# Attention with a window and sinks, then a gated MLP, on one core: another order of TensorE's groups, another load order, and other constants in the planner

## The chip, the core and the metric

The kernel runs on one core of one Trainium2 chip. The metric is the device time of one execution in microseconds, as the median over several runs. The profile is of one further execution; its span runs from the first to the last instruction of the program that the profiler recorded.

## What is computed

Four batches of eight heads, 768 tokens each, 64 channels per head. A token attends to the first four tokens (the sinks) and to the 128 tokens up to itself. The result, 3072 tokens of 512 channels, goes through an MLP with 2048 hidden channels whose gate is h * sigmoid(beta * h).

```python
scores = scale * np.matmul(q, k.transpose(0, 1, 3, 2))
is_sink = pos[None, :] < int(n_sink)
rel = pos[:, None] - pos[None, :]
keep = is_sink | ((rel >= 0) & (rel < int(window)))
scores = np.where(keep, scores, -1000000000.0)
a = np.exp(scores - np.max(scores, axis=-1, keepdims=True))
a = a / (np.sum(a, axis=-1, keepdims=True) + 1e-09)
x = np.matmul(a, v)            # then heads side by side: (3072, 512)
h = x @ w_in                   # (3072, 2048)
g = h * (1.0 / (1.0 + np.exp(-beta * h)))
out = g @ w_out                # (3072, 512)
```

Inputs and output are float32; the kernel multiplies in bfloat16.

## The kernel before

The tokens are cut into eight half-batches of 384. A half-batch has four units, one for each pair of heads. For the first two half-batches (`XB` is 2) TensorE transposes q and k, by identity products (function `T`, L697), and also transposes the attention output (`OT`, L880). For the other six a transposing DMA on SyncE does both (`XT` L734, `XO` L891).

One unit goes through these steps. Loads of q, k and v land in float32 staging tiles, of which each name has two (L635). Casts make bfloat16 of them, on VectorE, ScalarE or GpSimd (L558, L560, L563). Score products use 64 rows of the array, so those of the two heads run side by side (`SC`, L783). ScalarE takes the exponential (L792); masks are multiplied on VectorE (L803, L809) or selected on GpSimd (L798). The sinks' scores for later tokens have a product and an exponential of their own (`SS`, L819, L823), whose keys GpSimd gathers (L725). The attention-value products (`AV`, L851, L861) carry a column of ones, so that the row sums come with them; VectorE takes the reciprocal (L866) and normalises (L868).

The MLP has two products. The first (`HQ`, L910) makes 128 hidden channels of 384 tokens in four matmuls of 384 columns; ScalarE takes a tanh (L915) and VectorE forms the gate product (L917). The second (`OQ`, L931) accumulates 128 tokens of output over 16 matmuls of 512 columns in four groups. A copy with a factor of one half brings the result to SBUF, on ScalarE (L558) or VectorE (L564), and SyncE stores it (L940). The weights arrive in sixteen pieces of 512 KB (`load_w`, L647) and are cast, too.

Nothing is issued in the order in which this code stands. Each operation is recorded in a graph with its engine or choice of engines, an assumed duration, and what it reads and writes. TensorE's work is recorded in groups, each with a letter: T transposes, C and D the two halves of a unit's scores, S sinks, A attention-value, X output transposes, h and g the two halves of four first-product matmuls in the first two half-batches, H the same in the others, O a quarter of an output tile, b the transpose of beta. The string `ORDER` says in which order the groups come. The list `PAR['l0']` permutes the eleven loads of the first half-batch; the string `PAR['mix']` says how the loads of the next two half-batches (a) and the weight pieces (w) alternate. Loads are chained in that order on SyncE's queue.

`schedule` then walks in an assumed time. The next TensorE group, in the given order, and the next operation of every other engine compete by the earliest assumed start. Where several are ready on an engine, the one with the longest tail goes first. Where an operation can run on several engines, the one that would end first takes it, with a handicap for ScalarE (`BIAS` until `EARLY`). `place` gives each operation its assumed end, and each DMA an issue, a place in the stream and a landing. Where TensorE would idle before the assumed time 48 us (`FILL_TO`), `fillers` puts in products of ones (L1027), whose length is the assumed gap; up to 4.9 us they are assumed to run at half speed. What comes out of the walk is fixed: each engine's list, its engine choices, the PSUM banks and the fillers. On the chip each engine runs its list in order and waits on semaphores only.

Of the kernel before, what the change touches and what calls it, by code (L numbers as in the profile page):

```python
# [22 lines left out]
PAR = {'MD': 1, 'XB': 2, 'l0': [0, 2, 6, 1, 3, 4, 9, 5, 7, 10, 8], 'mix': 'aawwaawawawwawwaaaawwawwawwwawaa'}  # L23
ORDER = ('TCDTSTTDCSDSCASCTADACbXXAhhhXXThghDghgDhggThgggChhgghgShDSghSghghTghgCASCAXADOXOAhhhhXOXOgOOggOOhghg'
         'hhgOOOghgghghhhghgOgOSDgSChCOghSgADODCCOODOOSAAOAOSSOCCSOSODCHHHHHHHHOHDDOHAHDCHHAHHHAAOODDOOOODCDOH'
         'SCCHHOOASSHHOHOHHHHHSHHHAACSHSOHDCCOAODDOOCCDOAOOHHSHSAOHHOHAAHHHHHHHSHOHOHOSSOCDOHDCCOHHAOOHHHHHSHH'
         'HOSOCCDOHHOHODDAHOAHAOODCCASOOOCDDHHHHHHOAOHOOSHHOOSAHHAOHHHHHOOOHHHHOOHHHHHHOOHHHHOHOOOOOHOOOOOOOOO'
# [10 lines left out]
class Op:  # L38
    __slots__ = ("eng", "fn", "deps", "signal", "count", "waits", "sem", "vc", "dma", "seq", "end", "ns", "alts",
                 "group", "tail", "preds", "left", "succ", "at", "queue", "ring", "lag", "x", "tag", "chain")  # L40
# [6 lines left out]
class Graph:  # L47
# [4 lines left out]
    LEAD, PAD, LATE = 1500, 2000, 90000  # L52
    BIAS, EARLY = 300, 100000
    FILL_TO = 48000
    RING, FETCH, SWITCH = 165, 900, 85
    DEPTH = 9

    def __init__(self):
        self.ops = []
        self.groups = []  # L60
        self.writers = {}
        self.readers = {}
        self.last_load = None
        self.filler = None
# [7 lines left out]
    def add(self, eng, fn, ns=0, r=(), w=(), x=(), dma=None, alts=None, queue=470, ring=64, lag=0, after=(), tag=None):  # L72
# [4 lines left out]
        o.queue, o.ring, o.lag, o.x, o.tag, o.chain = queue, ring, lag, list(x), tag, None  # L77
# [28 lines left out]
    def place(self, o, at):  # L106
        o.at = at
        if o.dma:
            self.pending = [x for x in self.pending if x[0] > at]
            issued, need = at + o.queue + 40, min(o.ring, self.RING)  # L110
            total = sum(n for _, n in self.pending)
            for f, n in self.pending:
                if total + need <= self.RING:
                    break
                issued, total = max(issued, f), total - n
            begin = issued + o.lag if o.lag else at + 1150 + o.ns
            self.dma_free = max(self.dma_free + o.ns, begin)
            self.pending.append((self.dma_free, o.ring))
            self.free[o.eng] = issued
            o.end = self.dma_free + 950 + (self.PAD if at > self.LATE else 0)  # L120
        else:
            if o.eng == "pe":
                self.n_pe += 2
                if self.n_pe >= self.fetched + 256:
                    self.fetched += 256
                    self.dma_free = max(self.dma_free, at) + self.FETCH
                rows = o.group is not None and o.group.tag in "CD"
                if rows != self.rows:
                    at = o.at = at + self.SWITCH
                    self.rows = rows  # L130
            self.free[o.eng] = at + o.ns
            o.end = at + o.ns + self.LAT[o.eng]
# [15 lines left out]
    def schedule(self, order):  # L148
# [47 lines left out]
        self.dma_free, self.pending, self.n_pe, self.rows, self.fetched = 0.0, [], 0, False, 0  # L196
# [40 lines left out]
        while at_pe < len(todo) or pool:  # L237
# [20 lines left out]
            for o in pool:  # L258
                opts = []
                for e, (fn, ns) in o.alts.items():  # L260
# [5 lines left out]
                    if o.dma:  # L266
# [188 lines left out]
def _program(nc, G, sb, ps, q, k, v, w_in, w_out, beta, out):  # L455
# [274 lines left out]
    def XT(hb, i):  # L730
# [5 lines left out]
            x16[n][hb % NX][:, cs[0]:cs[0] + len(cs), :, :].rearrange("p c h d -> p (c h d)")), 1500,  # L736
            r=[(n + "16", hb % NX, j, c_) for j in range(4) for c_ in cs],
            w=[("qkT", hb % (NT // 4), j, i, c_) for j in range(4) for c_ in cs], dma=f"dx{n}{hb % 2}", queue=1540, ring=999, lag=1350)
# [25 lines left out]
    def SC(u):  # L764
# [23 lines left out]
        for j, grp in enumerate(gs):  # L788
# [5 lines left out]
            for kind_, sg in (("d", 1), ("p", -1)):  # L794
                at_ = [i for i, blk in enumerate(grp) if blk[0] == kind_]
                if at_:
# [5 lines left out]
                    if UNITS[u][0] < PAR.get('MD', 2):  # L802
                        alts["dve"] = (lambda e, d=d, mk=mk: e.tensor_tensor(d, d, mk, ALU.mult),  # L803
                                       70 + 256 * len(at_) / 1.9)
                    any_of(alts, r=[("E", z, j), ("maskT", int(kind_ == "p"))], w=[(kind_, z, j)])
            if grp[0][0] == "s":
# [3 lines left out]
                any_of({"gp": (fn, 1150), "dve": (fn, 335)}, r=[("E", z, j), "maskS"], w=[("s", z, j)])  # L810
# [252 lines left out]
```

The softmax here doesn't subtract the row's maximum and nothing guards it: scores larger than these inputs give would overflow.

## Time and profile before

| | |
|---|---|
| median of 5 runs | 226.73 us (226.5 to 227.06) |
| profiled execution, its own time | 227.1 us |
| its span | 225.4 us |
| TensorE busy | 217.8 us |
| VectorE busy | 142.2 us |
| ScalarE busy | 141.9 us |
| GpSimd busy | 67.0 us |
| first product of the MLP, 512 matmuls (L910) | 92.8 us busy, 326 ns mean |
| second product, 400 matmuls (L931) | 93.1 us busy, 371 ns mean |
| fillers, 31 matmuls (L1027) | 10.6 us busy |
| DMA | 40.95 MB, 182 GB/s on average |

Busy time is the union of the intervals in which instructions of a group were in flight. Consecutive matmuls overlap in flight, so a group's mean is longer than the spacing at which its matmuls are issued; the spacing is read from the starts in the timeline. "Idle before" is the engine's idle time just ahead of an instruction, followed by what released it.

### The profile page before, as it was taken

To read this page: it belongs to the slowest core of one execution; us is meant where nothing else is said; L and a number is where in the kernel's file an instruction comes from. 1 tells how busy PE (TensorE), PEld (TensorE's weight loads), DVE (VectorE), ACT (ScalarE), POOL (GpSimd) and SP (SyncE) were. 2 spreads that over 40 slices of the span, in tenths; PEclk is the share of its full clock that TensorE was granted. 3 is DMA by queue.
4 is the path that set the end of the run, shared out by engine and by line. 5 is a ranking of instruction groups with operands and counts; after the bars stand their busy time and mean duration, and the time that the engine had idled before them with its cause. 6 is when DMAs were issued, how large, how long until landed. Compare 5 with 4: busy or idle time off the path is not lost.

```text
span 225.4 us, 4484 instructions
## 1 busy us (share of the span) xinstructions
PE 217.8 (97%) x1720; PEld 119.5 (53%) x1720; DVE 142.2 (63%) x313; ACT 141.9 (63%) x257; POOL 67.0 (30%) x157
## 2 busy tenths in 40 slices
PE   8987999999999999999999999999999999999994
PEld 2544555555455445645564665455455556555443
DVE  2898899878758279839775478757362626455100
ACT  2595998145782767547788847778756756566221
POOL 7274344100363526352108510141435400000000
PEclk9999999999999999999999999999999999999999
DMA  7999979996999999899999999994133032101112
GB/s 161 266 345 373 351 188 348 344 248 126 216 204 213 226 203 235 192 251 223 202 237 203 201 224 220 247 242 118 47 84 81 0 84 81 49 4 47 47 47 93
DMA packets 104741, 40.95 MB, mean 182 GB/s; under 512 B 93312, under 2 KB 97680, under 8 KB 104720
## 3 DMA queue, kind: packets, MB, share of 16 engines
q1 hardware_dynamic: 103152, 40.65, 78.1%
q8 instruction: 13, 0.21, 0.4%
q10 hardware_dynamic: 1568, 0.02, 0.4%
q14 instruction: 8, 0.07, 0.1%
HBM read 27.30 MB, written 6.29 MB: 149 GB/s over the span
## 4 chain that ended last, share of the span: by engine, by line
PE 70%; DVE 10%; SPq 9%; DMA 9%; ACT 1%; issue 1%
PE P L931 32%; PE P L910 28%; SPq L635 6%; DVE g L917 4%; DMA wst<-in_moe_w_in_dram 4%; PE P L861 4%; PE P L783 3%; DMA k_stage<-in_k_dram 3%; DMA v_stage<-in_v_dram 2%; PE P L851 1%; DVE k L563 1%; DVE w_in L563 1%; SPq L891 1%; PE P L819 1%; DVE qkT L563 1%
## 5 line engine op out<-in xcount | busy, mean ns | idle before, releaser
L931 PE MATMUL P<-w_out,g 128*128 128x512 bf16 (+2 forms) x400 | 93.1, 371 | 0.1
L910 PE MATMUL P<-xT,w_in 128*128 128x384 bf16 x512 | 92.8, 326 | 0.3 <-DVE xT L563 0.3
L915 ACT ACTIVATE t<-P,hbeta 128x384 f32<-128x384 f32 x128 | 71.8, 587 | 31.7 <-PE P L910 24.5
L917 DVE SCALAR_TENSOR_TENSOR g<-t,P 128x384 bf16<-128x384 f32 x128 | 68.1, 550 | 35.2 <-ACT t L915 32.3
L798 POOL TENSOR_SCALAR_AFFINE_SELECT E<-E 128x256 bf16<-128x256 bf16 (+1 forms) x109 | 52.8, 516 | 57.6 <-ACT E L792 57.4
L910 PEld LDWEIGHTS P<-xT,w_in 128*128 128x128 bf16 x512 | 48.3, 98 | 35.2 <-issue 0.8
L931 PEld LDWEIGHTS P<-w_out,g 128*128 128x128 bf16 x400 | 36.6, 98 | 37.1 <-issue 1.1
L792 ACT ACTIVATE E<-P 128x768 bf16<-128x768 f32 (+1 forms) x64 | 45.6, 761 | 14.1 <-PE P L783 13.8
L861 PE MATMUL P<-vaug,E 128*128 128x65 bf16 x352 | 18.6, 193 | 0.7 <-DVE E L803 0.4
L558 ACT ACTIVATE osb<-P 128x512 f32<-128x512 f32 (+2 forms) x16 | 9.1, 571 | 15.3 <-PE P L931 15.1
L861 PEld LDWEIGHTS P<-vaug,E 128*128 128x128 bf16 x352 | 16.5, 97 | 3.9 <-ACT E L792 0.7
L868 DVE TENSOR_TENSOR onorm<-P,rden 128x384 bf16<-128x384 f32 x32 | 17.5, 553 | 0.5
L783 PE MATMUL P<-qkT 64*128 64x128 bf16 (+1 forms) x256 | 16.5, 239 | 1.1 <-ACT E L792 0.4
L823 ACT ACTIVATE ES<-P 128x128 bf16<-128x128 f32 (+1 forms) x32 | 12.1, 392 | 7.0 <-PE P L819 7.0
L563 DVE CAST k<-k_stage 128x512 bf16<-128x512 f32 (+1 forms) x24 | 11.8, 494 | 5.3 <-DMA k_stage<-in_k_dram 5.2
L783 PEld LDWEIGHTS P<-qkT 64*128 64x128 bf16 x256 | 8.2, 94 | 12.4 <-issue 4.4
L563 DVE CAST q<-q_stage 128x512 bf16<-128x512 f32 (+1 forms) x19 | 9.6, 504 | 6.5 <-DMA q_stage<-in_q_dram 6.5
L851 PE MATMUL P<-vS,ES 128*128 128x130 bf16 x64 | 12.7, 221 | 0.7 <-DVE vS L686 0.4
L563 DVE CAST vaug<-v_stage 128x512 bf16<-128x512 f32 x18 | 8.0, 442 | 8.0 <-DMA v_stage<-in_v_dram 7.9
L725 POOL TENSOR_TENSOR kS<-qkT,headm 128x8 bf16<-128x8 bf16 x16 | 3.0, 209 | 32.1 <-DMA qkT<-k 28.5
L1027 PE MATMUL P<-ones 128*128 128x512 bf16 (+2 forms) x31 | 10.6, 474 | 1.2 <-POOL ones L569 1.1
L564 DVE TENSOR_SCALAR osb<-P 128x512 f32<-128x512 f32 x9 | 6.2, 690 | 6.3 <-PE P L910 2.6
(48 smaller groups left out, 91.0 us busy)
## 6 DMA issues: line engine op xcount, KB each, us to landing
v_stage<-in_v_dram SPq DMA_DIRECT2D x24, 256.0 KB, 4.8
out_dram<-osb SPq DMA_DIRECT2D x23, 256.0 KB, 2.5
q_stage<-in_q_dram SPq DMA_DIRECT2D x18, 256.0 KB, 4.8
k_stage<-in_k_dram SPq DMA_DIRECT2D x18, 256.0 KB, 5.6
wst<-in_moe_w_in_dram SPq DMA_DIRECT2D x5, 512.0 KB, 8.5
wst<-in_moe_w_out_dram SPq DMA_DIRECT2D x4, 512.0 KB, 7.9
g<-in_moe_w_out_dram SPq DMA_DIRECT2D x4, 512.0 KB, 7.1
q_stage<-in_q_dram SPq DMA_DIRECT2D x8, 192.0 KB, 4.6
```

The lines of the kernel that those rows point to most:

```text
L563: return lambda e: e.tensor_copy(dst, at())
L635: o = add("sp", lambda e: e.dma_start(dst, src), ns, w=[("stg", n, z, j) for j in keys], dma=f"d{n}{z}{'' if i is None else i}", ring={610 ...
L783: add("pe", lambda e, dst=dst, own=own, kc=kc, rows=rows, q0=q0, nq=nq: e.matmul(dst(), tokens(own, hp, 1, rows, kc, 1)[:, 0, :], tokens(h ...
L792: add("act", lambda e, src=src, dst_=dst_: e.activation(dst_, src(), AF.Exp, bias=0.0, scale=SCALE), act_ns(256 * n), w=[(k_, z, j) for k_ ...
L798: alts = {"gp": (lambda e, d=d, sg=sg, at_=at_: e.affine_select(d, d, [[0, 2 * len(at_)], [sg, 128]], ALU.is_ge, 0.0, base=min(sg, 0), cha ...
L851: add("pe", lambda e, m=m, o0=o0: e.matmul(A()[:, o0:o0 + 2 * (D + 1)], ES[z][:, (c0 + m) * 128:(c0 + m + 1) * 128], vS[b % 2][:, 2 * hp:2 ...
L861: e.matmul(A()[:, o0:o0 + D + 1], E[z][:, i, hh, :], vaug[vz][:, kb % NK, 2 * hp + hh, :], start=a, stop=o, skip_group_check=True), 39,
L868: add("dve", lambda e: e.tensor_tensor(onorm[:, on, 2 * c0:2 * c1, :], av()[:, :, 0:D], rden[on][:, 0:2 * nb].unsqueeze(2).to_broadcast([1 ...
L910: first = add("pe", lambda e, c=c: e.matmul(hp(), w_in16[:, c, m * 128:(m + 1) * 128], xT[:, hb, c, 128 * c0:128 * c1], start=(c == 0), st ...
L915: add("act", lambda e: e.activation(tt[ti][:, 0:n], hp(), AF.Tanh, bias=0.0, scale=hbeta[:, m:m + 1]), act_ns(n) + 93, r=["hbeta"], w=[("t ...
L917: add("dve", lambda e: e.scalar_tensor_tensor(gt[hb % NG][:, m, 128 * c0:128 * c1], tt[ti][:, 0:n], 1.0, hp(), ALU.add, ALU.mult), dve_ns( ...
L931: add("pe", lambda e, m=m: e.matmul(P[:, bk[0], a:b], gt[hb % NG][:, m, t * 128:(t + 1) * 128], w_out16[:, m, a:b], start=(m == 0), stop=( ...
```

## The change

The order string, the load order and the alternation of loads are replaced. The planner's assumptions are replaced with them: a DMA's issue time now depends on the kind of the one before it (`DMA`, `CLASS`, `last_dma`), each kind has a service time, a queue room and a lag, fetches of instructions stall the assumed DMA stream at listed counts on all engines (`FETCHES`, `SMALL`, `stall`), some assumed durations of masks, attention-value products and transposing loads are altered, and `DEPTH`, `LEAD`, `BIAS` and `EARLY` have other values. A choice of the engine that issues the stores is added (`OUT`), which nothing sets.

The operations on the data are the same in number and size. The built lists differ on all engines: 45 fillers instead of 31; 34 runs of consecutive score groups (C or D) instead of 37; full-size output copies on VectorE 2 instead of 9 and on ScalarE 21 instead of 14; some casts of q, k, v and of weights on other engines; and the order everywhere. The order begins with `TTSCD` instead of `TCDTS`, and the first eleven loads are k1 q3 q1 k0 q0 v0 v1 k3 q2 k2 v2 instead of q0 q1 q3 k0 k1 q2 v1 k2 k3 v2 v0, where the number is a pair of heads for q and k and a block of 128 tokens for v. In TensorE's list the first transpose stands behind 20 fillers of 512 columns and one of 256; before it was behind 12 and one of 384.

```diff
-PAR = {'MD': 1, 'XB': 2, 'l0': [0, 2, 6, 1, 3, 4, 9, 5, 7, 10, 8], 'mix': 'aawwaawawawwawwaaaawwawwawwwawaa'}
-ORDER = ('TCDTSTTDCSDSCASCTADACbXXAhhhXXThghDghgDhggThgggChhgghgShDSghSghghTghgCASCAXADOXOAhhhhXOXOgOOggOOhghg'
-         'hhgOOOghgghghhhghgOgOSDgSChCOghSgADODCCOODOOSAAOAOSSOCCSOSODCHHHHHHHHOHDDOHAHDCHHAHHHAAOODDOOOODCDOH'
-         'SCCHHOOASSHHOHOHHHHHSHHHAACSHSOHDCCOAODDOOCCDOAOOHHSHSAOHHOHAAHHHHHHHSHOHOHOSSOCDOHDCCOHHAOOHHHHHSHH'
-         'HOSOCCDOHHOHODDAHOAHAOODCCASOOOCDDHHHHHHOAOHOOSHHOOSAHHAOHHHHHOOOHHHHOOHHHHHHOOHHHHOHOOOOOHOOOOOOOOO'
+PAR = {'MD': 1, 'XB': 2, 'l0': [3, 6, 2, 1, 0, 8, 9, 7, 4, 5, 10], 'mix': 'waaawwawaaawwwawaaawwawwwwaawwaa'}
+ORDER = ('TTSCDTTDCCSSCADDSXAATXCAbDSXhhXhTgghgghghghghCThhgDgghhgghSTDhSChghgSgAADAXCXOhOOAghhOXXOggOhhOggOhg'
+         'hOhhghgOghOhggghghgOhghDggDCOSOCCDOSOSACDAOOSAOOOASSOSOSOCDCHHHHHHHHCHAHDDOOCDHHHAAHHHOAOOODDSODCCOS'
+         'OOHCDHASSHAHHHCOHAOHHHHOHHSHAHHOOODCCOOSDCDOHHHCDAAHHOHOSHHHHAOHSHOCAOCDCHHHSOHDDSOSHHOOHHHHCDOSSHAO'
+         'OHOAOAHAHSOCCDHHHHOAHHOHOOCDDOHOOHASSOOAOODCHHHHHOHOAHOHHHHOHOHHOOHHHHHHOHOOOHHHHOHOHOHHOOOOOOOOOOOO'
...
-    LEAD, PAD, LATE = 1500, 2000, 90000
-    BIAS, EARLY = 300, 100000
+    LEAD, PAD, LATE = 2000, 2000, 90000
+    BIAS, EARLY = 200, 45000
...
-    RING, FETCH, SWITCH = 165, 900, 85
-    DEPTH = 9
+    FETCH, SHORT, SWITCH = 1150, 400, 85
+    SMALL = {"sp": (42, 80), "dve": (50, 180), "gp": (56,), "act": (193,)}
+    CLASS = {"out": 0, "nat": 1, "hb": 1, "xt": 2, "xo": 3, "w": 4, "pair": 4, "dual": 4, "beta": 4}
+    DMA = {"nat": ((434, 580, 580, 580, 470), 64, 1140, 115, 2250), "hb": ((434, 580, 580, 580, 470), 64, 2290, 115, 3390),
+           "out": ((335, 580, 580, 335, 367), 8, 650, 110, 950), "w": ((434, 580, 580, 580, 468), 16, 1370, 108, 2470),
+           "pair": ((434, 580, 580, 580, 468), 16, 600, 113, 1700), "dual": ((434, 580, 580, 580, 468), 32, 1160, 113, 2260),
+           "beta": ((434, 580, 580, 580, 468), 1, 190, 113, 1000), "xt": ((1367, 1440, 1420, 1440, 1440), 128, 1280, 17, 0),
+           "xo": ((1212, 1287, 1287, 1212, 1287), 60, 720, 66, 920)}
+    DEPTH = 8
+    FETCHES = (152, 232, 368, 477, 608, 730, 858, 988, 1111, 1222, 1354, 1482, 1601, 1728)
...
-        o.queue, o.ring, o.lag, o.x, o.tag, o.chain = queue, ring, lag, list(x), tag, None
+        o.queue, o.ring, o.lag, o.x, o.tag, o.chain, o.first = queue, ring, lag, list(x), tag, None, dma and dma not in self.sems
+        self.sems.add(dma)
...
+        e = o.eng
+        self.count[e] = self.count.get(e, 0) + 1
+        if self.count[e] in self.SMALL.get(e, ()):
+            self.stall(at, self.SHORT)
...
-            self.pending = [x for x in self.pending if x[0] > at]
-            issued, need = at + o.queue + 40, min(o.ring, self.RING)
-            total = sum(n for _, n in self.pending)
-            for f, n in self.pending:
-                if total + need <= self.RING:
+            kind = self.kind(o)
+            quick, n, svc, room, lag = self.DMA[kind]
+            self.pending = [x for x in self.pending if x[1] > at]
+            wait, total = at, sum(x[2] for x in self.pending)
+            for b, f, m, _ in self.pending:
+                if total <= room:
...
-                issued, total = max(issued, f), total - n
-            begin = issued + o.lag if o.lag else at + 1150 + o.ns
-            self.dma_free = max(self.dma_free + o.ns, begin)
-            self.pending.append((self.dma_free, o.ring))
-            self.free[o.eng] = issued
-            o.end = self.dma_free + 950 + (self.PAD if at > self.LATE else 0)
+                total -= m
+                if total <= room:
+                    wait = max(wait, f - (f - b) * (room - total) / m)
+                    break
+            prev, start = self.last_dma
+            issued = max(at + quick[prev], wait, start + 2370 if prev == 2 else 0)
+            self.last_dma = (self.CLASS[kind], at)
+            self.n_dma += 1
+            svc += {2: 150, 3: 80, 0: 60}.get(prev, 0) if kind == "nat" else 60 if kind == "xt" and prev == 0 else 0
+            f = max(self.dma_free + svc, at + 3090 if kind == "xt" else issued + lag)
+            f += 450 if self.n_dma in (2, 3) else 800 if o.dma == "do0" and o.first else 0
+            f += 700 if o.dma == "dw0" and o.first else 0
+            self.pending.append((max(self.dma_free, f - svc), f, n + 1, o))
+            self.dma_free = f
+            self.free[e] = issued + 43
+            o.end = f + 600 + (self.PAD if at > self.LATE else 0)
...
-            if o.eng == "pe":
-                self.n_pe += 2
-                if self.n_pe >= self.fetched + 256:
-                    self.fetched += 256
-                    self.dma_free = max(self.dma_free, at) + self.FETCH
+            if e == "pe":
+                self.n_pe += 1
+                if self.n_pe in self.FETCHES:
+                    self.stall(at, self.FETCH)
...
-            self.free[o.eng] = at + o.ns
-            o.end = at + o.ns + self.LAT[o.eng]
+            self.free[e] = at + o.ns
+            o.end = at + o.ns + self.LAT[e]
+
+    def kind(self, o):
+        for k, v in (("dx", "xt"), ("dy", "xo"), ("do", "out"), ("dw", "w"), ("dbeta", "beta")):
+            if o.dma.startswith(k):
+                return v
+        return {16: "pair", 32: "dual"}.get(o.ring, "hb" if o.ns > 2000 else "nat")
+
+    def stall(self, at, ns):
+        self.pending = [x if x[1] <= at else (x[0], x[1] + ns) + x[2:] for x in self.pending]
+        for x in self.pending:
+            if x[1] > at + ns:
+                x[3].end += ns
+        self.dma_free = max(self.dma_free, at) + ns
...
-        self.dma_free, self.pending, self.n_pe, self.rows, self.fetched = 0.0, [], 0, False, 0
+        self.dma_free, self.pending, self.n_pe, self.rows, self.n_dma = 0.0, [], 0, False, 0
+        self.count, self.last_dma = {}, (4, -9999.0)
...
-                    if o.dma:
+                    if o.dma and e == "sp":
...
-            x16[n][hb % NX][:, cs[0]:cs[0] + len(cs), :, :].rearrange("p c h d -> p (c h d)")), 1500,
+            x16[n][hb % NX][:, cs[0]:cs[0] + len(cs), :, :].rearrange("p c h d -> p (c h d)")), 1250,
...
-            w=[("qkT", hb % (NT // 4), j, i, c_) for j in range(4) for c_ in cs], dma=f"dx{n}{hb % 2}", queue=1540, ring=999, lag=1350)
+            w=[("qkT", hb % (NT // 4), j, i, c_) for j in range(4) for c_ in cs], dma=f"dx{n}{hb % 2}", queue=1450, ring=999, lag=1350)
...
-                                       70 + 256 * len(at_) / 1.9)
+                                       150 + 256 * len(at_) / 1.6)
...
-                any_of({"gp": (fn, 1150), "dve": (fn, 335)}, r=[("E", z, j), "maskS"], w=[("s", z, j)])
+                any_of({"gp": (fn, 1150), "dve": (fn, 430)}, r=[("E", z, j), "maskS"], w=[("s", z, j)])
...
-                                 start=a, stop=o, skip_group_check=True), 39,
+                                 start=a, stop=o, skip_group_check=True), 36,
...
-            ring=60, lag=700)
+            ring=60, lag=580)
...
-            any_of(copies(osb[z][:, a:b], lambda: P[:, bk[0], a:b], {"dve": dve_ns(b - a), "act": act_ns(b - a)}, 0.5), w=[("osb", z)],
-                   x=[(bk, 0)])
-            add("sp", lambda e: e.dma_start(out_t[NK * hb + t][:, a:b], osb[z][:, a:b]), 640 * (b - a) // NOUT, r=[("osb", z)],
+            ways = {"dve": dve_ns(b - a), "act": act_ns(b - a)}
+            if PAR.get('OUT', "sp") == "act" and T_ < len(TILES) - 1:
+                del ways["dve"]
+            any_of(copies(osb[z][:, a:b], lambda: P[:, bk[0], a:b], ways, 0.5), w=[("osb", z)], x=[(bk, 0)])
+            add(PAR.get('OUT', "sp"), lambda e: e.dma_start(out_t[NK * hb + t][:, a:b], osb[z][:, a:b]), 640 * (b - a) // NOUT, r=[("osb", z)],
```

More of the change, by code (lines that the diff above doesn't have):

```diff
@@ L39 @@
     __slots__ = ("eng", "fn", "deps", "signal", "count", "waits", "sem", "vc", "dma", "seq", "end", "ns", "alts",
-                 "group", "tail", "preds", "left", "succ", "at", "queue", "ring", "lag", "x", "tag", "chain")
+                 "group", "tail", "preds", "left", "succ", "at", "queue", "ring", "lag", "x", "tag", "chain", "first")
 class Group:
@@ L63, in __init__ @@
         self.last_load = None
+        self.sems = set()
         self.filler = None
```

## Prediction

> **What bounds the kernel now.** I read the page first, then TensorE's rows of the timeline (early and late), then the engines' busy time by stretch, then the one group that writes the masks on VectorE.
>
> ```profile
> span 225.4 us, 4484 instructions
> PE 217.8 (97%) x1720; PEld 119.5 (53%) x1720; DVE 142.2 (63%) x313; ACT 141.9 (63%) x257; POOL 67.0 (30%) x157
> ```
>
> TensorE sets the time, but 97% is no work share: a row runs from its first start to its last end, and an end comes some 0.16 us after the next matmul may start. What counts is start to start. TensorE's timeline, late:
>
> ```profile
> 119.51 1.03 PE L931 MATMUL P<-w_out,g 128*128 128x512 bf16 x4
> 120.47 0.50 PE L783 MATMUL P<-qkT 64*128 64x256 bf16 x8
> 120.91 1.90 PE L931 MATMUL P<-w_out,g 128*128 128x512 bf16 x8
> 122.74 0.67 PE L783 MATMUL P<-qkT 64*128 64x256 bf16 x12
> ```
>
> Eight 512-column matmuls take 122.74 - 120.91 = 1.83 us with the change of form at their end. In the chain of waits eight of them take 1.73 us (0.216 each) and eight 384-column ones 1.30 us (0.163 each). So the four from 119.51 are done at 120.375 and the score matmuls (64 rows, two side by side) start 0.095 later. Their 4 pairs need 0.33 us (0.110 for a pair with 256 columns, 0.056 for one with 128), to 120.80, and the next form starts 0.11 later. One run of score groups therefore costs about 0.19 us in changes of form, whatever is in it.
>
> The same timeline, early:
>
> ```profile
> 6.47 0.38 PE L697 MATMUL P<-ident,q 128*128 128x128 bf16 x3
> 6.76 0.34 PE L697 MATMUL P<-ident,k 128*128 128x128 bf16 x3
> 6.94 1.46 PE L1027 MATMUL P<-ones 128*128 128x512 bf16 x6
> 8.33 0.45 PE L783 MATMUL P<-qkT 64*128 64x256 bf16 x8
> ...
> 19.12 0.77 PE L1027 MATMUL P<-ones 128*128 128x512 bf16 x3 [0.17 <-DVE onorm L868]
> 19.73 1.14 PE L910 MATMUL P<-xT,w_in 128*128 128x384 bf16 x6
> ...
> 22.28 0.66 PE L910 MATMUL P<-xT,w_in 128*128 128x384 bf16 x3 [0.25 <-DVE xT L563]
> ```
>
> L1027 is filler: products of ones that keep the array busy. The first real matmul is at 6.47, the first of the MLP at 19.73.
>
> The ledger of the 225.4 us, by counts and starts: 1.06 before the first matmul; real matmuls 197.5 (512 of L910 at 0.163 = 83.2; L931 at 0.216, with 16 each of 384 and 128 columns, 83.0; attention-value products 352 at 0.029 and 64 at 0.057 = 13.9; score pairs 80 at 0.056 and 48 at 0.110 = 9.8; sinks and transposes 7.7); 37 score runs at 0.19 = 7.0; filler 9.0 (5.41 before 6.47, then 16.75 units of 512 columns at 0.216 = 3.6); 3.0 after the last matmul starts; and, as the rest, **7.8 of waits**. Of these 3.7 lie before 19.73, about 4.1 behind it.
>
> Why it waits is in the busy time by stretch (the columns are PE, PEld, DVE, ACT, POOL), and in the group that multiplies by the mask:
>
> ```profile
> 9.80:23.30 13.50, 11.37 (x136) 6.73 (x135) 11.30 (x30) 10.58 (x21) 7.66 (x16) 1.00 1.10 345
> 23.30:42.00 18.70, 17.96 (x175) 10.45 (x174) 18.51 (x40) 15.45 (x28) 8.43 (x15) 1.00 1.00 296
> 42.00:60.00 18.00, 18.00 (x105) 9.45 (x104) 14.10 (x30) 8.42 (x16) 0.67 (x4) 1.00 0.94 222
> ```
>
> VectorE is busy 18.51 of 18.70 us from 23.3 to 42: there it is the bound beside TensorE.
>
> ```profile
> L803 DVE TENSOR_TENSOR E<-E,maskT x3: 279/916/1020, 15.1 to 17.7; 128x256 bf16<-128x256 bf16 x3
> ```
>
> **What the Trainium skill says.** "TensorE: Matmul & The Clock Gate", section "What's actually happening": the clock starts at half rate and rises after a busy window of about 3.4 us that runs freely, so the moment differs from run to run. The trace agrees: fillers come every 0.427 us until about 6.57 us, then every 0.216. "SBUF — State Buffer", section "SBUF: two separate sides": VectorE with two SBUF inputs and GpSimd exclude each other for a whole instruction. The trace agrees: the same mask product takes 0.28 us alone, and 0.92 and 1.02 while GpSimd works.
>
> **The change part by part.** No real operation is added or removed. The constants of the planner, the order string and the load order make another list for each engine.
>
> *Fillers.* 31 become 45: 39 of 512 columns, four of 256, one each of 384 and 128. Twenty and a half units now stand before the first transpose (12.75 before). At the clock of the trace 13 run slow (1.06 to 6.61), then 7 and a half at 0.216 each: the first transpose is at 8.23 us. Its data would be there at about 7.45: it needs the fifth load now, and in the trace the cast of the fifth load runs 6.92 to 7.34. Price: 7.17 instead of 5.41. The other 21.5 units cost 4.65 instead of 3.62. If the clock rises earlier, at 4.9, the first transpose comes at about 7.45 instead.
>
> *Score runs.* 37 become 34: 3 x 0.19 = 0.57 less.
>
> So without waits the new span is 1.06 + 7.17 + 4.65 + 197.5 + 6.46 + 3.04 = 219.9, against 217.6 of before. The new order loses 2.3 us for certain and must have 2.3 us fewer waits than 7.8 to break even: at most 5.5.
>
> *Waits in front.* Both v loads needed first now come ahead of the last k and q; the last k that the third and fourth transposes need is the tenth load, not the ninth. Walking the new lists with durations of the trace: transposes 8.23 to 8.91; VectorE's copy of the first (0.94) to 9.82; sink keys on GpSimd, first scores at about 10.3 (8.33 before). Eight fillers to 12.46. VectorE does two sink copies, a v cast, two casts and a mask before the last k cast, which ends at about 12.4, so the third transpose waits little. The exponentials follow on ScalarE from 10.75 instead of 8.71. The first output transpose then waits for VectorE (copy to 14.3, mask, weight cast 0.69, mask, reciprocal, masked product, normalisation 0.55) until about 17.1 where TensorE is free at 15.7; the second and third attention products wait for masks of GpSimd. First MLP matmul: about 21.7, with 0.35 us more real work behind it than before. 1.06 + 7.17 + 4.1 of filler + 6.75 of work and changes leave 2.6 of waits, against 3.7.
>
> *Waits behind it.* VectorE's list up to the first gate product (L917) has 2 k casts, a transpose copy and a weight cast more and 2 v casts fewer: 1.01 + 0.95 + 0.69 - 0.87 = 1.8 us more. But up to the 32nd it has less: two output copies (1.4), two mask products (0.9), two v casts (0.9), a transpose copy (0.95), a q cast (0.5), a w_out cast (0.7) and small ones (0.5) fewer, a w_in cast (0.7) more: 5.2 us less. ScalarE and GpSimd take much of it; ScalarE has 15.45 busy of 18.70 in the fullest stretch, GpSimd 8.43. So the waits that the timeline blames on VectorE between 22 and 42 (0.42, 0.33 and 0.35, with 0.26 on ScalarE), and those on gate products at 83 and 85 (0.25, 0.43), lose most of their cause. A wait of 0.44 at 73.9 for the transposing k load shrinks too: the first group that needs that k stands 1.1 us of TensorE work later. I take 2.2 for 4.1; some 1.5 is small change that no order has removed.
>
> *Loads.* Bytes are the same. Two transposing loads of k now stand behind another transposing load, which holds SyncE 1.3 us; the cover is the work before their first reader, and without it each costs up to 1.3. Output copies move from VectorE (9 to 2 of full size) to ScalarE, 0.57 instead of 0.69 each, under TensorE's work.
>
> *Sum.* 219.9 + 2.6 + 2.2 = 224.7, against 225.4. The profiled execution took 227.1, so 1.7 lies around its span: 226.4; the median of the runs, 226.73, is 0.37 below it. Forecast 226.0.
>
> **The rivals.** (a) The front is not late: VectorE and ScalarE catch up before the MLP begins. Then waits are 1.4 in front and 1.8 behind: 223.1, time 224.4. For it: gaps on ScalarE in the front; against: VectorE's longer list. (b) Slower: VectorE becomes the bound of the front. Its 1.8 us more work, with mask products at 1.0 instead of 0.3 beside GpSimd, brings the first MLP matmul to 23.4 and front waits to 4.3; with 2.8 behind, 227.0, time 228.3. It decides from a first MLP matmul later than about 22.4. (c) The waits only move: 5.5 remain, and the time is 226.7. (d) A transposing load comes late once or twice behind the one it now follows: 1.2 us on top of the forecast, 227.2; against it, TensorE reaches most k later.
>
> **How the numbers follow.** Forecast 0.40 (its own range 225.1 to 226.9), (a) 0.16, (b) 0.20, (c) 0.13, (d) 0.11. Within 0.2% (226.28 to 227.18), about what this measurement tells from no change, lie a fifth of the forecast, most of (c) and a fifth of (d): 0.19. Faster: most of the forecast and (a), 0.47. Slower: (b), most of (d) and the edges, 0.34. The range leaves out the ends of (a) and (b): 224.4 to 228.2.
>
> **What would show it.** First transpose at 8.2 and first MLP matmul near 21.7; first gate product near 24; VectorE less than full between 24 and 42; waits behind the front of about 2; 34 score runs. A first MLP matmul after 22.4, a new wait for a transposing load, or gate products that still end TensorE's waits would make it wrong.

## The result, and the profile after

The kernel after takes 227.99 us, median of 24 runs (227.29 to 229.81), beside 226.97 of the kernel before in 43 runs: a ratio of 1.005, 95% interval 1.0034 to 1.0066. It is slower by about 1.0 us. Three executions of kernels further below, of 322.05, 791.86 and 237.63 us, stand apart from the others of their kernel and are left out of the times. The forecast was 226.0, with a range of 224.4 to 228.2: the time lies within the range, on the other side of the old time than the forecast.

The profiled execution of the kernel after took 228.53 us, 1.4 more than that of before; each was profiled once more later (227.53 and 226.22, with spans of 225.8 and 224.5).

The page's first part, of the kernel after (span; busy time, share and instructions of each engine):

```profile
span 226.8 us, 4511 instructions
PE 218.6 (96%) x1734; PEld 120.6 (53%) x1734; DVE 136.9 (60%) x301; ACT 145.3 (64%) x265; POOL 72.9 (32%) x161
```

VectorE does 5.3 us less than before, ScalarE 3.4 and GpSimd 5.9 more. So work did leave the engine that was named as the bound beside TensorE, and the time still rose.

TensorE's timeline of the kernel after, early (start, length, line, operation, tiles, count, and in brackets the idle time before it with what ended it):

```profile
8.19 0.33 PE L735 MATMUL P<-ident,q 128*128 128x128 bf16 x3
...
17.43 0.34 PE L918 MATMUL P<-ident,onorm 128*128 128x128 bf16 x3 [0.52 <-DVE onorm L906]
...
21.30 0.81 PE L948 MATMUL P<-xT,w_in 128*128 128x384 bf16 x4
```

The first transpose came at 8.19 (foretold 8.23), the first MLP matmul at 21.30 (foretold about 21.7, before 19.73). In the second profile of after they came at 7.42 and 20.82. VectorE's mask products, which took 0.28, 0.92 and 1.02 us before, are these now:

```profile
L841 DVE TENSOR_TENSOR E<-E,maskT x3: 270/351/380, 12.3 to 17.8; 128x256 bf16<-128x256 bf16 x3
```

So none of them came near the 1.0 us that the slower rival (b) needed, and the front came in a little under its number.

The busy time by stretch, of the kernel after (columns PE, PEld, DVE, ACT, POOL as before):

```profile
9.80:23.30 13.50, 12.08 (x154) 7.62 (x153) 11.52 (x31) 11.47 (x22) 9.61 (x19) 1.00 1.09 350
23.30:42.00 18.70, 17.12 (x157) 9.77 (x156) 17.02 (x36) 15.05 (x28) 8.20 (x13) 1.00 1.05 319
42.00:60.00 18.00, 18.00 (x115) 9.98 (x114) 12.43 (x26) 9.33 (x18) 0.91 (x1) 1.00 0.86 193
```

From 23.3 to 42 VectorE is down from 18.51 to 17.02 us. It is less than full, as foretold; but TensorE is down as well, from 17.96 to 17.12. A lower busy time is not yet a relief: it is also lower where an engine waits, and where it has come less far in its list.

The ledger of the prediction, with the counts and starts of the trace after: 1.06 + 7.13 (filler before the first transpose) + 4.65 (other filler) + 197.5 + 34 x 0.19 = 6.46 + 3.04 = 219.9 without waits, the foretold number. The rest of 226.8 is 6.9 of waits. In front 21.30 - 1.06 - 7.13 - 4.1 - 6.75 = 2.3 (foretold 2.6); behind it 4.6 (foretold 2.2; before 4.1). The same sum over the second profiles gives 4.2 behind the front for after and 3.5 for before. One correction: the order string has 34 runs of score groups, but fillers at 13.46 cut one of them in two on TensorE. With 35 changes of form the waits are 6.7, and those in front 2.1.

Where the time went shows in places at which both orders have placed the same groups. "To 19.40" means that the next group starts at 19.40. The starts are those of the second profiles, of before and after:

| stretch, by groups placed | before | after | after minus before |
|---|---|---|---|
| to the 25th | to 19.40 | to 20.20 | +0.80 |
| 25th to 56th | to 29.30 | to 29.88 | -0.22 |
| 56th to 93rd | to 45.89 | to 47.84 | +1.37 |
| 93rd to 153rd | to 72.94 | to 74.06 | -0.83 |
| 153rd to 160th | to 75.71 | to 77.56 | +0.73 |
| 160th to 180th | to 88.01 | to 89.09 | -0.77 |
| 180th to the last | to 221.22 | to 222.52 | +0.22 |

Each large entry has a reading. **To the 25th**: the first transpose comes 0.95 later (7.42 for 6.47), and in this profile it waits for the cast of its load (0.26 of idle time), not for filler. **93rd to 153rd**: two score runs fewer (4 for 6, 2 x 0.19 = 0.38) and the wait for a transposing load of k at 72.9 (0.41) gone: 0.79 of 0.83. **160th to 180th**: the waits on gate products at 82.1 and 83.8 (0.25 and 0.53 in this profile) gone: 0.78 of 0.77. **153rd to 160th**: a transposing load of k arrives late. These last two belong together. In four profiles of kernels with the same lists there (below) the load is not late, and the 153rd to the 160th take 2.75 us instead of 3.50; but then a wait of some 0.3 to 0.4 for a gate product comes back at about 82. The two stretches together take 14.8 to 14.9 there, against 15.0 to 15.1 in both profiles of after and both of before. **56th to 93rd** is the largest loss. TensorE there, in the first profile of after:

```profile
32.95 0.34 PE L821 MATMUL P<-qkT 64*128 64x256 bf16 x4 [0.24 <-ACT qkT L596]
33.65 1.47 PE L948 MATMUL P<-xT,w_in 128*128 128x384 bf16 x8 [0.36 <-ACT E L830]
36.30 0.19 PE L899 MATMUL P<-vaug,E 128*128 128x65 bf16 x1
37.19 0.27 PE L899 MATMUL P<-vaug,E 128*128 128x65 bf16 x3 [0.70 <-DVE vaug L601]
...
40.41 0.60 PE L969 MATMUL P<-w_out,g 128*128 128x512 bf16 x2 [0.27 <-DVE w_out L601]
```

Counted from start to start (with a change of form where one falls in), the four waits are 0.42, 0.54, 0.87 and 0.43 us, 2.26 together. The kernel before had 0.40, 0.43 and 0.35 = 1.18 in the same stretch. The difference of 1.08 and half a filler more (0.11) make 1.19 of the 1.37.

The wait of 0.87 is the longest; in before the same v cast was waited for, too, but 0.35. VectorE's timeline of after shows what the v cast (L601) stood behind:

```profile
33.30 0.76 DVE L601 CAST vaug<-v_stage 128x512 bf16<-128x512 f32 x2
35.56 0.56 DVE L955 SCALAR_TENSOR_TENSOR g<-t,P 128x384 bf16<-128x384 f32 x1 [1.50 <-ACT t L953]
36.03 1.10 DVE L601 CAST vaug<-v_stage 128x512 bf16<-128x512 f32 x1
```

The third v load of this half-batch had landed at 32.50. Its cast could have followed the other two at 34.06. It stands behind the gate product, which waited 1.50 us for a tanh; and once it ran, it took 1.10 us, the two before it 0.42 each. GpSimd was at work beside it on a weight cast:

```profile
35.81 1.04 POOL L598 TENSOR_SCALAR_AFFINE_SELECT w_out<-wst 128x1024 bf16<-128x1024 f32 x1
```

The second profile has the same pair: 1.10 again, and GpSimd's cast ends some 0.28 before the v cast in both. At 0.42 the cast would have ended at 36.45 instead of 37.13, and of the 0.87 some 0.2 would be left; that is an estimate from these starts and lengths. Why the tanh (L953) was late is in ScalarE's timeline of after:

```profile
32.02 0.88 ACT L596 ACTIVATE qkT<-P 128x768 bf16<-128x768 bf16 x1
32.71 1.59 ACT L830 ACTIVATE E<-P 128x768 bf16<-128x768 f32 x2
34.09 0.97 ACT L861 ACTIVATE ES<-P 128x384 bf16<-128x384 f32 x2
34.84 0.70 ACT L953 ACTIVATE t<-P,hbeta 128x384 f32<-128x384 f32 x1
```

A copy, two exponentials and two sink exponentials run without a gap from 32.0 to 34.8. The two waits at 32.9 and 33.6 are on this engine too. It was about as full in before, where it had no gap over 0.16 from 23.0 to 36.0; what is new is what stands ahead of the tanh.

### The profile page after: what moved, and what is told of

Same layout as the page of the kernel before. It is cut to its first block, busy times and chain, and to the rows that moved or that the text cites. A ratio compares the mean times of both kernels' runs of the same rounds, so it can differ in the third digit from the quotient of the medians.

```text
span 226.8 us, 4511 instructions
## 1 busy us (share of the span) xinstructions
PE 218.6 (96%) x1734; PEld 120.6 (53%) x1734; DVE 136.9 (60%) x301; ACT 145.3 (64%) x265; POOL 72.9 (32%) x161
## 4 chain that ended last, share of the span: by engine, by line
PE 82%; DMA 6%; ACT 5%; DVE 4%; issue 1%; SPq 0%; POOL 0%; POOLq 0%
PE P L969 33%; PE P L948 33%; PE P L1067 5%; PE P L821 5%; PE P L899 4%; DMA v_stage<-in_v_dram 4%; DMA qkT<-k 2%; ACT t L953 2%; ACT E L830 2%; PE P L889 1%; PE P L857 1%; DVE onorm L906 1%; PE P L735 1%; ACT qkT L596 1%; DVE g L955 1%
## 5 line engine op out<-in xcount | busy, mean ns | idle before, releaser
L948 PE MATMUL P<-xT,w_in 128*128 128x384 bf16 x512 | 93.8, 326 | 0.4 <-ACT E L830 0.4
L953 ACT ACTIVATE t<-P,hbeta 128x384 f32<-128x384 f32 x128 | 71.9, 591 | 32.6 <-PE P L948 29.6
L836 POOL TENSOR_SCALAR_AFFINE_SELECT E<-E 128x256 bf16<-128x256 bf16 (+1 forms) x109 | 56.1, 544 | 75.9 <-ACT E L830 75.7
L596 ACT ACTIVATE osb<-P 128x512 f32<-128x512 f32 (+2 forms) x23 | 13.3, 579 | 20.9 <-PE P L969 20.8
L821 PE MATMUL P<-qkT 64*128 64x128 bf16 (+1 forms) x256 | 16.0, 239 | 1.7 <-DMA qkT<-k 0.8
L601 DVE CAST k<-k_stage 128x512 bf16<-128x512 f32 (+1 forms) x22 | 11.8, 541 | 4.4 <-DMA k_stage<-in_k_dram 4.4
L1067 PE MATMUL P<-ones 128*128 128x512 bf16 (+3 forms) x45 | 13.1, 437 | 1.1 <-POOL ones L607 1.1
L601 DVE CAST q<-q_stage 128x512 bf16<-128x512 f32 (+1 forms) x20 | 10.5, 526 | 5.5 <-DMA q_stage<-in_q_dram 5.5
L847 DVE TENSOR_TENSOR E<-E,maskS 128x512 bf16<-128x512 bf16 x16 | 8.0, 497 | 7.0 <-ACT E L830 6.9
L598 POOL TENSOR_SCALAR_AFFINE_SELECT vaug<-v_stage 128x512 bf16<-128x512 f32 x6 | 4.2, 708 | 21.0 <-DMA v_stage<-in_v_dram 21.0
L904 DVE RECIPROCAL rden<-P 128x6 f32<-128x6 f32 x32 | 5.9, 188 | 8.0 <-PE P L899 7.9
```

Source lines behind the costliest of these rows:

```text
L596: return lambda e: e.activation(dst, at(), AF.Copy, bias=0.0, scale=scale)
L601: return lambda e: e.tensor_copy(dst, at())
L821: add("pe", lambda e, dst=dst, own=own, kc=kc, rows=rows, q0=q0, nq=nq: e.matmul(dst(), tokens(own, hp, 1, rows, kc, 1)[:, 0, :], tokens(h ...
L836: alts = {"gp": (lambda e, d=d, sg=sg, at_=at_: e.affine_select(d, d, [[0, 2 * len(at_)], [sg, 128]], ALU.is_ge, 0.0, base=min(sg, 0), cha ...
L948: first = add("pe", lambda e, c=c: e.matmul(hp(), w_in16[:, c, m * 128:(m + 1) * 128], xT[:, hb, c, 128 * c0:128 * c1], start=(c == 0), st ...
L953: add("act", lambda e: e.activation(tt[ti][:, 0:n], hp(), AF.Tanh, bias=0.0, scale=hbeta[:, m:m + 1]), act_ns(n) + 93, r=["hbeta"], w=[("t ...
```

## The experiments

Three theories stood against each other. **A**: the loss is made of single waits at a few places, chiefly the v cast behind the gate product. **B**: the late front does it (twenty and a half units of filler before the first transpose). **C**: a transposing load behind another does it. A fourth question was whether order or constants are to blame.

### The v cast ahead of the gate product

In the list of after, one cast moves one place up on VectorE (`up` moves an operation past its engine's neighbours, `tagged` finds it; both are used below):

```
     G.schedule(ORDER)
+    up(G, tagged(G, "cast", 1, "v", 2), 1)
```

> The changed kernel with the third v cast of the second half-batch one place earlier on VectorE, ahead of the gate product that waits for ScalarE's tanh. Blocked-cast theory: the wait of 0.87 us at 37.2 disappears (the load landed at 32.5), and the time falls by 0.6 to 0.9 us. Theory that waits only move: the wait for the w_out cast behind it (0.43 at 40.4) grows by as much, and the time falls by 0.3 or less.

Measured: 227.19 us in 22 runs, 1.0017 of before (0.9999 to 1.0036); the interval of after, 1.0034 to 1.0066, barely touches this one. VectorE's timeline:

```profile
32.87 1.53 DVE L617 CAST vaug<-v_stage 128x512 bf16<-128x512 f32 x3
35.13 0.56 DVE L971 SCALAR_TENSOR_TENSOR g<-t,P 128x384 bf16<-128x384 f32 x1 [0.73 <-ACT t L969]
```

All three casts run in one piece and end at 34.40, while VectorE would wait anyway, and the gate product's own wait shrinks to 0.73. TensorE's wait of 0.87 is gone, the next one fell from 0.43 to 0.21, and the stretch from the 56th to the 86th group took 14.05 us instead of 14.92. So mending this one place gives back 0.8 us, nearly as much as the change lost, as theory A said; the edit moves nothing else. Two limits: 0.35 of this wait was in the kernel before, too, so the change lost only some 0.5 us by it; and the move takes the cast away from GpSimd's weight cast as well as out from behind the gate product (at its new place, beside GpSimd's masks, it took 0.86 us, but nobody waited), so the shares of the two are not told apart.

### Shorter filler before the first transpose

Three units of 512 columns and one of 256 are removed in front of the first transpose, 0.76 us at full clock:

```
     G.schedule(ORDER)
+    for p in [p for p in G.ops if p.eng == "pe" and p.group is None][17:21]:
+        G.ops.remove(p)
...
```

> The changed kernel without the last three fillers of 512 columns and the one of 256 ahead of the first transpose; nothing else differs. Late-start theory: the first transpose comes at 7.4 to 7.5 us instead of 8.19, the first MLP matmul 0.5 to 0.7 earlier than 21.30, and the time falls by 0.5 to 0.7 us against the changed kernel. Theory that blocked casts behind the front decide: the front moves as much, but the weight and v loads do not, so at least half of it is lost again in the waits at 37 and 40 us, and the time falls by 0.3 or less.

Measured: 228.3 us in 8 runs, 1.0071 (1.0045 to 1.0098): no gain. TensorE's timeline:

```profile
7.67 0.34 PE L754 MATMUL P<-ident,q 128*128 128x128 bf16 x3 [0.43 <-DVE q L620]
```

The transpose starts 0.52 us sooner than in the first profile of after, but now it waits for the cast of the load: the front is held by its loads until about 7.4 to 7.7 in any case. In the second profile of after the first transpose came at 7.42 with all the filler in place, and across the profiled executions of after's order it lies between 7.42 and 8.19. Theory B, as a matter of too much filler, falls. That the front is later by some 0.8 stays (the 25th group is passed at 20.2 to 20.7, in before at 19.4 to 19.7), and no run took that away by itself.

### Copies of ScalarE and transposing loads

Two smaller waits of the first profile of after were taken on in the same way. First ScalarE's v cast of the seventh half-batch, put one place later, ahead of which TensorE had waited 0.64 at 140.7:

```
+    up(G, tagged(G, "cast", 6, "v", 2), -1)
```

> The changed kernel with ScalarE's v cast of the seventh half-batch, which waits for its load until 139.3 us, one place later, behind the exponential that stands ready. Blocked-cast theory: the wait of 0.64 us at 140.7 shrinks to 0.1 or disappears, and the time falls by 0.4 to 0.7 us. Theory that waits only move: the v cast, 0.7 later now, delays the attention products that read it, and the time stays within 0.2.

Measured: 227.81 us in 11 runs, 1.0044 (1.0019 to 1.0069), 0.2 under after, which is no difference. The expected 0.4 to 0.7 did not come. The wait is gone from this profile; but with the same list there it was 0.20 in the second profile of after, about 0.74 with the shorter filler, and nothing with the moved v cast. It comes and goes by itself, so its absence isn't shown to be the work of this edit.

Then the late load of k. In after, the last two k casts of the fourth half-batch stand on VectorE behind a reciprocal that waits for TensorE, and the transposing load of this k behind another transposing load. Both were turned round:

```
+    up(G, tagged(G, "cast", 3, "k", 1), 2)
+    up(G, tagged(G, "cast", 3, "k", 2), 2)
+    up(G, next(p for p in G.ops if p.dma == "dy0"), -1)
```

> The changed kernel with the last two k casts of the fourth half-batch moved ahead of the reciprocal that waits for TensorE at 70.6 us on VectorE, and the transposing load that reads them moved ahead of the other transposing load. Blocked-cast theory: the load is issued near 70.9 instead of 72.1 and lands near 75.5 to 76.5 instead of 77.4; the wait of 0.94 at 77.5 shrinks to 0.1 to 0.3, and the time falls by 0.5 to 0.8 us. Theory that a fetch of instructions holds it anyway: it lands at 77 or later, and the time stays within 0.3.

Measured: 228.58 us in 17 runs, 1.007 (1.0051 to 1.0088): 0.6 more than after, not less. Its profiled execution is the one of 322.05 us, so whether the wait went away isn't known from this run. What the second profile of after has there is this:

```profile
76.96 0.67 PE L821 MATMUL P<-qkT 64*128 64x256 bf16 x12 [0.69 <-DMA qkT<-k]
```

It is 0.85 from start to start, and 0.94 in the first profile; in the profiles of the kernels with the shorter filler, with the moved v cast, with ScalarE's cast put later and with the moved copy (below), whose lists are the same here, there is no wait. The load itself took 5.31 and 5.22 us from issue to landing in the two profiles of after and 3.64 to 3.67 in these four, behind the same other transposing load; in the two of before it took 3.71 and 3.70. So standing behind another transposing load is not what made it long, and theory C falls as it was put; what the long ones have in common is in the last section.

All four edits together:

> The changed kernel with four edits: the shorter filler in front, the v cast earlier on VectorE, the v cast later on ScalarE, and the last two k casts of the fourth half-batch ahead of the reciprocal that waits for TensorE, with the transposing load that needs them ahead of the transposing load before it. If the losses are separate: the sum of the parts, 2.0 to 2.8 us below the changed kernel, which is 1.0 to 1.8 below the kernel before. If waits only move: less than 1.0 below the changed kernel.

Measured: 227.39 us in 22 runs, 1.0026 (1.0008 to 1.0043), 0.6 below after and no better than the v cast alone; the losses don't add up as separate ones. Its TensorE timeline shows a wait that none of the others had:

```profile
76.00 0.50 PE L972 MATMUL P<-xT,w_in 128*128 128x384 bf16 x2
77.32 1.96 PE L972 MATMUL P<-xT,w_in 128*128 128x384 bf16 x11 [0.82 <-DMA xT<-onorm]
```

The k load, moved ahead, landed in 3.78 us; the load that was put back, issued at 71.14, wasn't late either. Late is the transposing load after it, issued at 73.09: it took 4.19 us, and 2.76 with the v cast alone.

### Is the rest of that stretch ScalarE's order?

With the v cast moved, TensorE still waits 0.42 and 0.54 on ScalarE (at 32.5 and 33.2 in its profile). On top of it the copy of the transposed q and k was put one place earlier on ScalarE, ahead of a tanh:

```
+    up(G, tagged(G, "cast", 1, "v", 2), 1)
+    up(G, tagged(G, "qkT", 1, 3), 1)
```

> The changed kernel with the v cast earlier and, on ScalarE, the copy of the eighth transposed q and k one place earlier, ahead of a tanh that nobody waits for yet. If ScalarE's order holds TensorE at 32.5 and 33.2 us (0.42 and 0.53 of waits): these shrink by 0.2 to 0.4, and the time is 0.2 to 0.5 below that with the v cast alone, near 226.8. If ScalarE's total holds it: no change against the v cast alone.

Measured: 227.98 us in 22 runs, 1.0051 (1.0032 to 1.007): 0.8 slower than the v cast alone. TensorE's timeline:

```profile
33.49 0.34 PE L838 MATMUL P<-qkT 64*128 64x256 bf16 x3 [0.72 <-DVE g L972]
```

The tanh that was passed leads to the gate product that this score group now waits for. Two waits with a sum of 0.96 became one of 0.95, and small waits behind it grew: the 56th to the 93rd group took 17.58 us, against 17.08 with the v cast alone. Swapping the two instructions doesn't help; that ScalarE's total is the limit here is the likely reading, but no run took work from it at this place.

### The same cast in the kernel before

There TensorE waited 0.35 us for the same v cast. It was given to GpSimd in the list of before:

```
+    o, to = tagged(G, "cast", 1, "v", 2), tagged(G, "cast", 1, "v", 1)
...
+    o.eng, (o.fn, o.ns) = "gp", o.alts["gp"]
+    G.ops.remove(o)
+    G.ops.insert(G.ops.index(to) + 1, o)
...
```

> The kernel before with the third v cast of the second half-batch on GpSimd, which idles when the load lands, instead of on VectorE, which is full there. If this one cast bounds TensorE around 35.7 us in both kernels: the wait of 0.35 us there disappears and the time falls by 0.3 to 0.8 us below the kernel before. If VectorE's total bounds that stretch: less, 0.1 to 0.4, as VectorE loses 0.43 of work. If waits only move: no change.

Measured: 226.68 us in 14 runs, 1.0001 of before (0.9979 to 1.0024). In the profile the 56th to the 93rd group took 16.26 us, against 16.66 and 16.59 in the two of before, and the whole rest from the 56th on 191.5 to the last group's start, against 192.1 and 191.9. The ratio of the times shows no gain, but its interval reaches down to 0.5 us less, so whether the 0.35 was won can't be told from them.

### Order or constants

Three kernels crossed the two halves of the change. The old order and load order with the new planner constants:

```
-PAR, ORDER (after)
+PAR, ORDER (before)
```

> The planner of the changed kernel with the group order and the load order of before. If the new group and load order make it slower, this is at or below the kernel before (226 to 227). If the planner's constants do, through other engine choices and fillers, this is as slow as the changed kernel or slower (228 or more).

Measured: 229.4 us in 9 runs, 1.0094 (1.0066 to 1.0123). The new order and loads with the old constants and queue model (the same edit on the kernel before, with the strings of after):

> The planner of before with the new group order and load order. If the new order is slower by itself, this is at least as slow as the changed kernel (228 or more). If the constants are the cause, this is at or below the kernel before. An order made for one planner may also do badly with the other in both mixed kernels; then both are slower than either original.

Measured: 235.66 us in 5 runs, 1.0354 (1.0311 to 1.0398). The 25th group is passed only at 21.67 us there. Last, the first 25 groups and the first loads of before, and all else from after:

```
-'l0': [3, 6, 2, 1, 0, 8, 9, 7, 4, 5, 10]
+'l0': [0, 2, 6, 1, 3, 4, 9, 5, 7, 10, 8]
-ORDER = ('TTSCDTTDCCSSCADDSXAATXCAbDSXhhXhT...
+ORDER = ('TCDTSTTDCSDSCASCTADACbXXADSXhhXhT...
```

> The changed kernel with the first 25 groups and the first eleven loads of before; these 25 groups are the same set in both orders. Late-start theory: the first transpose comes near 6.5, the 26th group at or before 20.0 instead of 20.7, and the time falls by 0.7 or more. Blocked-cast theory: the front gains, but the time falls by less than 0.5, since the same loads and casts are waited for at 37 and 77 us.

Measured: 231.1 us in 5 runs, 1.0173 (1.0137 to 1.0208). The first transpose moved up to 6.11 us, and the 25th group was still passed at 20.32, no sooner than after's 20.20 to 20.69. So this run doesn't test a kernel with an early front: from 14.5 on nine fillers stand ahead of the fifth group of transposes, and a wait for a k cast in it; in before this group starts at 14.47.

```profile
14.49 2.06 PE L1067 MATMUL P<-ones 128*128 128x512 bf16 x9
16.39 0.33 PE L735 MATMUL P<-ident,q 128*128 128x128 bf16 x3
17.45 0.34 PE L735 MATMUL P<-ident,k 128*128 128x128 bf16 x3 [0.73 <-DVE k L601]
```

The alternation of the later loads (`mix`) was still that of after; whether that is why is not shown.

For the front the crossed kernels do tell the two halves apart, by one profile of each and two of before and after: the 25th group is passed at 19.40 and 19.73 in before, at 18.78 with the old strings and the new constants, at 21.67 with the new strings and the old constants, and at 20.20 and 20.69 in after. With either set of constants the new strings make the front later, by 1.4 to 2.3 us, and with either strings the new constants make it earlier, by 0.6 to 1.5. Behind the front it is otherwise: from there to the end the crossed kernels take 209.1 and 212.3 us, before and after 205.1 to 206.1. Each order with the other's constants is worse than either kernel, so behind the front the loss can't be credited to one of the two.

### Both kernels once more

To see which waits return:

> The changed kernel once more, for a second profile. Waits that belong to the lists come again: 0.41, 0.53, 0.46 and 0.70 in front, 0.42 and 0.53 near 33, 0.87 near 37, 0.43 near 40. The waits of 0.94 at 77.5 (a transposing load) and 0.64 at 140.7 belong to that execution if they do not come again. The first transpose falls between 7.45 and 8.2 us, by where the array's clock rises.

> The kernel before once more, for a second profile. Waits that belong to the lists come again: those near 22.3, 30.6, 35.0 and 35.8. Those at 73.9, 83 and 85 may not. The first transpose falls near 6.5 us or a little earlier, and the first MLP matmul between 19.4 and 19.8.

Measured: 227.53 and 226.22 us. The place in question, TensorE, in the second profile of after and then of before:

```profile
35.81 0.19 PE L899 MATMUL P<-vaug,E 128*128 128x65 bf16 x1
36.71 0.27 PE L899 MATMUL P<-vaug,E 128*128 128x65 bf16 x3 [0.70 <-DVE vaug L601]
```

```profile
34.96 0.27 PE L861 MATMUL P<-vaug,E 128*128 128x65 bf16 x3 [0.18 <-DVE vaug L563]
```

The v cast's wait returns to the hundredth (0.70 of idle time), while the waits at 77 and 140.7 of after change and one at 22.3 of before (0.42) vanishes. The table above rests on these two profiles for that reason.

## Why the prediction was wrong in direction

*Right.* The fillers: the first transpose at 8.19 for 8.23, 7.13 of filler for 7.17, and 4.65 for 4.65. The 8.19 is in part luck: the second profile has 7.42, the case that the prediction gave for an earlier rise of the clock. The score runs: 34 in the order (35 on TensorE), and their price of 0.19 fits the 93rd to the 153rd group. The front: 21.30 for 21.7, waits of 2.3 for 2.6. The sum without waits, 219.9. The Trainium skill, page "TensorE: Matmul & The Clock Gate", section "What's actually happening", says that the moment of the clock's rise differs from run to run; the runs agree, with the first transpose at 8.19 and at 7.42 us in two executions of one program.

*Wrong.* The step "Waits behind it", with "I take 2.2 for 4.1": 4.6 were measured, and the missing 2.4 us are more than the foretold gain of 0.7. Three things failed in it.

The relief of VectorE was counted up to the 32nd gate product: 5.2 us less. That product lies at 63 to 64 us in both kernels, and the waits in question lie before 41. Counted by the median length of each kind of instruction over the four profiles, VectorE's new list has 36.7 us of work up to the 16th gate product (at 40.5 in before, 44.6 in after) where the old one has 35.8; and ahead of the v cast that TensorE waits for (at 35.3 and 36.0) it has 28.8 where the old one has 28.9. There was no relief there. It came after the place that needed it, where (42 to 60) TensorE was busy all the time already before.

And only totals were compared; which instruction stands behind which was not walked. The work taken from VectorE was ascribed to ScalarE and GpSimd as engines with room, on 15.45 busy of 18.70 in the whole stretch, while ScalarE is full from 32.0 to 34.8. So its tanh is late, the gate product waits, and the v cast behind it is late with its data long there. The moved cast shows that the end of this chain is worth 0.8 us; its beginning, on ScalarE, is read from the timelines only.

Third, a longer instruction beside GpSimd was kept for rival (b) and the masks of the front. One turned up behind the front, the v cast: 1.10 us instead of 0.42, with GpSimd's weight cast beside it. That GpSimd is the cause is the likely reading; no run took its cast away.

*The rivals.* (c), that waits only move, came nearest: with 6.9 of waits instead of its 5.5, so more came than went. What was foretold to fall at 73.9 did fall (0.41); on the gate products at 83 to 85 it fell in the two profiles of after (0.78), and some 0.3 to 0.4 of it was there in four others. New waits on ScalarE and a longer one on the v cast outweighed it. (b) named the mask products and a first MLP matmul after 22.4, and neither came. (d), a transposing load that comes late, was seen at 77 with 0.85 to 0.94, in two of six profiled executions with that stretch of list unchanged; the reason that it gave, the load in front, is not it.

*What stays open.* With the v cast moved, 227.19 us are left beside 226.96 of before in the same comparison, within the interval of no difference. The later front and the transposing load stand against fewer score runs and the waits that went, and none of these was tested alone with a gain. How the v cast's delay divides between its place and GpSimd, and whether ScalarE's total or its order makes the tanh late, stays open too. Of the tried kernels none beats the kernel before by a measurable amount.

## What to carry to other kernels

Sum an engine's work up to the place of the wait that is to go, not over the stage: 5.2 us less by the 32nd gate product was no less ahead of the cast that was waited for. Then walk the list at that place: look for a short instruction with its data ready that stands behind one waiting for another engine, and for what GpSimd does beside it; moving one such cast by one place gave back 0.8 us where the change had lost 1.0. And profile a kernel twice before a single wait is believed: some returned to the hundredth of a us, others came and went.

## What was not expected of the hardware

The transposing load of the fourth half-batch's k took 5.3 us from issue to landing in the first profile of after (72.08 to 77.39), 3.7 in that of before (70.06 to 73.76). In the long one a 16 KB instruction fetch of 0.96 us began at 75.19 on another queue, 3.1 us after the load's issue. The second profile of after has the same: a load of 5.22 and a fetch 2.9 after its issue. In the four profiles of kernels with the same lists there, the fetch began 4.8 to 4.9 us after the issue, when the load of 3.64 to 3.67 had landed. With all four edits together the fetch, at 75.08, fell into the next transposing load, and that one was late (4.19 instead of 2.76). So each long one of these loads had a fetch begin 2 us or more before it landed, and none of the short ones had. No run moved the fetch alone, and why it came earlier in after is not known.
